# Induced-set attention and a SwiGLU block on one core: Newton roots, one set of PSUM banks, and a new instruction order

## The chip, the core and the metric

The kernel runs on one core of a Trainium2 chip. The core has a matmul engine (TensorE, PE in the profile, with its weight loads as PEld), a vector engine (VectorE, DVE), an activation engine (ScalarE, ACT), a general engine (GpSimd, POOL) and a sequencer that here only issues transfers (SyncE, SP). Each engine takes its own instructions strictly in the order in which the program gives them, and waits on semaphores for the others. The metric is the device time of one execution in microseconds; lower is better.

## The reference

There are four batches of 12416 rows of 128 numbers. Each goes through two attention steps with 32 learned rows, and the result, taken as 49664 rows, through a gated block of width 1536:

```python
def mab(q, kv):
    s = scale * (q @ kv.transpose(0, 2, 1))
    s = s - s.max(-1, keepdims=True)
    a = np.exp(s)
    a /= a.sum(-1, keepdims=True) + 1e-09
    return a @ kv
h = mab(I, x)                       # I: the 32 learned rows, for each batch
x = mab(x, h).reshape(B * S, D)     # 49664 x 128
rms = np.sqrt(np.mean(x * x, axis=-1, keepdims=True) + 1e-06)
xn = x / rms * rms_g
g = xn @ w_gate                     # 128 x 1536
silu = g * (1.0 / (1.0 + np.exp(-g)))
return silu * (xn @ w_val) @ w_out  # 1536 x 128
```

All inputs are random. The weights come as float64 and are rounded to fp32 on the chip.

## The kernel before

**Blocks.** Each batch is cut into seven sets of columns (five of 2048 rows, one of 1920, one of 256), and these into 25 units: twenty of 512 rows, four of 480, one of 256. Each unit goes through the 12 slices of 128 of the inner width. That is 25 x 12 = 300 blocks a batch and 1200 in all. One block is a gate matmul (`gate`, line 682), SiLU on ACT (`silu`, 692; for some blocks a tanh on ACT, 689, and a product on DVE, 702), a value matmul (`value`, 710), their product on DVE (`times_value`, 724) and the projection onto 128 outputs. Weights of gate and value are folded with the attention's 32 rows into stacks `sg` and `sv` (lines 485 and 504), so that the attention's output itself is never formed: the moving operand `a` is the normalised attention weight, split in a high and a low half.

**Three kinds of projection.** A block's letter in the string `sorts` chooses its kind:

- P, plain: the product goes to SBUF, and one full fp32 matmul with `wo` (line 781, `project_plain`; it appears as two matmul records) adds it to the unit's output sum in PSUM.
- S, split: the product u stays in its PSUM bank. ACT makes a rounded high part (`high`, 737), DVE the scaled rest (`low`, 743). Two fp32r matmuls put high and low parts in the bank of the upper sum (`project_two`, 769 and 770). POOL adds high and low parts in place (`add_in_place`, 789), and a third fp32r matmul (`project_third`, through 781) adds that to the output sum.
- D: like S, with the product in SBUF, the rest on POOL (`low_of_u`, 750) and a second ACT step (`high_down`, 756).

The first 26 blocks (`EARLY`) are plain whatever the string says. When a unit's matmuls are done, ACT takes the upper sum (`take_upper`, 822), DVE adds the output sum (`finish`, 834) and transposes it (842), and SP stores it in four transfers (855).

**Attention for the next batch** runs between the blocks of the present one: transposes of x (323), scores (340), maxima (352 to 362), exponentials on ACT (371, 473), sums (392), the 32 rows h, their products with the weights (485), second scores (340, 458), row maxima and their subtraction (462, 466; on POOL, or on DVE for the first set). For each set a chain called `seam` normalises: a transpose (540), a matmul with the rows' Gram matrix (544), a product (550), sums (554, 555), the root, its product with the weights (564, POOL), a transpose (568) and the two halves (574, 580). The root is one instruction on POOL:

```python
def root():
    rs = st["rs"] = numbers("rs")
    nc.gpsimd.tensor_tensor(out=rs, in0=st["ms"], in1=mhalf[rows, 0:n], op=ALU.pow)   # line 560
```

**Memory.** The eight PSUM banks are divided: five (`ps_gv`) for gates, values, products that stay in PSUM and all of the attention; two (`ps_acc`) for output sums; one (`ps_u`) for upper sums. Split factors have 19 places in SBUF, named by the string `holders`.

**Order.** It is written out. A first stage, the string `ORDER`, handles batch 0's attention and the rounding of the first third of the weights (lines 256 to 286). A second (`early`) ties the rest of the rounding, the stacks and the second scores to the first 26 blocks by block number. The remaining order is the string `program` of some 10,500 letters: g, s, v, m, p, h, l, n, e, q, d, r for the steps above, E, F, T, O for a unit's end, a for the transfers that gather `a`, and a dot for the next step of attention, whose number stands in `taken`. Where several blocks wait for the same step, the oldest is taken. Which bank a matmul gets stands in the string `banks`.

Of the kernel before, what the change touches and what calls it, by code (L numbers as in the profile page):

```python
# [23 lines left out]
def kernel(  # L24
# [10 lines left out]

# [47 lines left out]
    outp = pool("outp", 2)  # L117
    ps_gv = pool("ps_gv", 1, space=PSUM)
    ps_acc = pool("ps_acc", 2, space=PSUM)
    ps_u = pool("ps_u", 1, space=PSUM)  # L120
# [41 lines left out]
    mhalf = const.tile([P, 16], F32, name="mhalf")  # L162
# [24 lines left out]
    def warm(n):  # L187
        ps = ps_acc.tile([P, 512], F32, name="acc")
        for _ in range(n):
            nc.tensor.matmul(ps[:, 0:P], ident[:], ident[:], start=True, stop=True)  # L190

    warm(7)
    ps = ps_gv.tile([P, 512], F32, name="gv", tag="gv4")
# [25 lines left out]
    w0 = {}  # L219

    def rounding(i, c):
# [4 lines left out]
        def put():  # L226
            if i < 2:
                nc.sync.dma_start(out=w32[i][c][:], in_=st["dst"])
            if unread:
                fetch_raw(*unread.pop(0))  # L230
# [11 lines left out]
        def power():  # L242
            if i < 2:
                t = (xnp.tile([P, 512], F32, name=f"xn{2 * c - 1 + i}") if c else
                     silp.tile([P, 512], F32, name="silu") if i else halves.tile([P, 512], F32, name="lo"))
                w0[i, c] = t[:]
                dst = st["dst"] = w0[i, c]
            else:
                dst = st["dst"] = wo.rearrange("p j c -> p (j c)")[:, ts(c, 512)]
# [16 lines left out]
        def upper():  # L266
            if wide:
                f = st["f"] = outp.tile([P, 512], I32, name="o")
                nc.vector.tensor_scalar(out=f[:], in0=st["high"], scalar1=0xFFFFF, scalar2=None, op0=ALU.bitwise_and)
# [11 lines left out]
        def lower():  # L281
            if wide:
                e, f = st["e"], st["f"].bitcast(F32)
                nc.vector.scalar_tensor_tensor(out=f[:], in0=st["low"].bitcast(U32), scalar=2.0 ** -52, in1=f[:],
                                               op0=ALU.mult, op1=ALU.add)
                nc.gpsimd.tensor_tensor(out=st["dst"], in0=f[:], in1=e.bitcast(F32)[:], op=ALU.mult)  # L286
            put()
# [6 lines left out]
    NB, turn, turns, works, factors = 5, [0], [], [int(c) for c in "01201212"], []  # L294

    def bank():
# [5 lines left out]
        return ps_gv.tile([P, 512], F32, name="gv", tag=f"gv{n}")  # L302
# [5 lines left out]
    def attention(b, load_next):  # L308
# [41 lines left out]
        def max1():  # L350
            t = st["own"] = small.tile([P, R, NS], F32, name="owns")
            nc.vector.tensor_tensor(out=t[:], in0=st["gmx"][:].unsqueeze(1).to_broadcast((P, R, NS)),
# [88 lines left out]
        def square_h():  # L441
# [3 lines left out]
            stacks[b] = [stk.tile([P, F], F32R, name=n) for n in ("sg", "sv")]  # L445
# [18 lines left out]
        def sub_max(s):  # L464
            n, v, mx = per2[s], weights(b, s), st["mx2", s]
            (nc.gpsimd if s else nc.vector).tensor_tensor(
# [29 lines left out]
        def place(i, k):  # L496
            half = st["halves", i][k // 2]
            for c in range(NC):
                nc.sync.dma_start(out=stacks[b][i][ts(k, m), ts(c, 512)].bitcast(F32), in_=half[ts(c, m), :].bitcast(F32))

        def stack_of(i, c):
# [3 lines left out]
            nc.scalar.copy(out=stacks[b][i][:, ts(c, 512)], in_=ps[:])  # L505
# [22 lines left out]
    def seam(b, s):  # L528
# [29 lines left out]
        def root():  # L558
            rs = st["rs"] = numbers("rs")
            nc.gpsimd.tensor_tensor(out=rs, in0=st["ms"], in1=mhalf[rows, 0:n], op=ALU.pow)  # L560
# [21 lines left out]
        return [turn_a, square, times, scale, root, apply, turn_b, split, lower]  # L582

    def gather(b, u):
# [4 lines left out]
        a = moving[b, u] = (xnp.tile([P, 512], F32R, name="xn0") if (b, u) == (0, 2) else  # L589
# [4 lines left out]
    def split_wo(step):  # L594

        if not step:
            kws["first"] = xnp.tile([P, half + NK, C], F32R, name=f"xn{full - 1}")
            rings = [xnp.tile([P, RING * 512], F32R, name=f"xn{full - 4 + n}") for n in range(3)]
            kws["room"] = [ring[:, ts(n, 512)] for ring in rings for n in range(RING)][:3 * RING - 2]
            kws["wide"], kws["own"] = rings[2], {}  # L600

        def part(kind, g):
            n = kind * NK + g * half
            t = kws["first"][:, n:n + half, :] if n < half + NK else kws["more"][:, n - half - NK:n - NK, :]
            return t, t.bitcast(F32)

        def scaled(kind, g, mul, src=None):
            to, now = part(kind, g)
            nc.scalar.activation(to, now if src is None else src, AF.Copy, scale=mul)

        for g in range(2):
            one = wo[:, g * half:(g + 1) * half, :]
            at = step - g
            if at == 0:
                scaled(0, g, 1.0 - 2.0 ** -13, one)
            if at == 1:
                nc.gpsimd.tensor_tensor(out=part(1, g)[0], in0=one, in1=part(0, g)[1], op=ALU.subtract)
            if at == 3:
                scaled(1, g, 4096.0)
            if at == 4:  # L620
                nc.gpsimd.tensor_tensor(out=part(2, g)[0], in0=part(0, g)[1], in1=part(1, g)[1], op=ALU.subtract)
            if at == 6:
                scaled(0, g, -4096.0)

    def last_of(step):

        n = NJ - NK
        room = rings_last()
        one, (whi, wlo, ws) = wo[:, NK:NJ, :], (room[:, ts(kind, n), :] for kind in range(3))
# [11 lines left out]
    def rings_last():  # L641
        return kws["wide"][:, 2 * 512:4 * 512].rearrange("p (k c) -> p k c", c=C)

    def weight_of(kind, j):
        if j >= NK:
            return rings_last()[:, kind * (NJ - NK) + j - NK, :]
        n = kind * NK + j
        return kws["first"][:, n, :] if n < half + NK else kws["more"][:, n - half - NK, :]

    blocks, kinds = [], []  # L650
    at_unit = {}
    lists = {name: [] for name in "hlneqdDrRpx"}
# [3 lines left out]
    def unit_of(b, u):  # L656
        if (b, u) not in at_unit:
            s, q = units[u]
            at_unit[b, u] = {"T": per2[s] * m, "a": moving.pop((b, u)), "left": NJ, "q": 0, "acc": None,
                             "k": sum(kind != "P" for kind, one in zip(kinds, blocks) if one[:2] == (b, u)), "ups": None,  # L660
                             "o": None}
# [6 lines left out]
    def factor():  # L668
        return up.tile([P, 512], F32, name="u", tag=f"u{factors.pop(0)}")

    def room():
        n = factors.pop(0)
        if n < HELD and n not in kws["own"]:
            kws["own"][n] = up.tile([P, 512], F32R, name="u", tag=f"u{n}")[:]
        return kws["own"][n] if n < HELD else kws["room"][n - HELD]
# [20 lines left out]
    def gate_times():  # L696
        n = lists["x"].pop(0)
# [14 lines left out]
    def times_value():  # L712
# [5 lines left out]
        else:  # L718
            factor_of[n] = {"u": factor()[:, 0:T]}
# [7 lines left out]
    def high():  # L727
        n = lists["h"].pop(0)
# [11 lines left out]
    def low():  # L740
        n = lists["l"].pop(0)
# [5 lines left out]
    def low_of_u():  # L747
        n = lists["n"].pop(0)
# [4 lines left out]
    def high_down():  # L753
        n = lists["e"].pop(0)
# [4 lines left out]
    def project_two():  # L759
        n = min(lists["q"], key=lambda n: blocks[n][:2])  # L760
        lists["q"].remove(n)
# [3 lines left out]
        if one["ups"] is None:  # L765
            one["ups"] = ps_u.tile([P, 512], F32, name="u3")
        ups = one["ups"][:, 0:T]
        last = one["q"] == one["k"] - 1
        nc.tensor.matmul(ups, weight_of(0, j), halves_in_turn(t["hi"]), start=not one["q"], stop=False)  # L769
        nc.tensor.matmul(ups, weight_of(1, j), halves_in_turn(t["lo"]), start=False, stop=last)  # L770
        one["q"] += 1
        lists["D" if kinds[n].islower() else "d"].append(n)

    def project(n, lhsT, rhs, step2):
# [3 lines left out]
        if one["acc"] is None:  # L778
            one["acc"] = ps_acc.tile([P, 512], F32, name="acc")
        to = one["acc"][:, 0:T]  # L780
        nc.tensor.matmul(to.rearrange("p (n h) -> p h n", h=2) if step2 else to, lhsT, rhs, start=one["left"] == NJ,  # L781
                         stop=one["left"] == 1)
# [3 lines left out]
    def add_in_place():  # L786
        n = lists["d"].pop(0)
# [4 lines left out]
    def add_by_transfer():  # L792
        n = lists["D"].pop(0)
        t = factor_of[n]
        nc.gpsimd.dma_start(out=t["lo"].bitcast(F32), in_=t["hi"].bitcast(F32), accum_op=ALU.add)
        lists["R"].append(n)

    def project_third(name):
        n = lists[name].pop(0)
        project(n, weight_of(2, blocks[n][2]), halves_in_turn(factor_of[n]["lo"]), False)  # L800

    def project_plain():
        n = lists["p"].pop(0)
# [4 lines left out]
    flat = [(b, u) for b in range(B) for u in range(NU)]  # L808
# [5 lines left out]
    def take_upper():  # L814
        b, u = next_unit("E")
        one = unit_of(b, u)
        T = one["T"]
        assert one["q"] == one["k"]
        if not one["k"]:
            return  # L820
        o = one["o"] = outp.tile([P, 512], F32, name="o")
# [3 lines left out]
    def finish():  # L825
# [4 lines left out]
        if not one["k"]:  # L830
            one["o"] = outp.tile([P, 512], F32, name="o")
        whole = one["o"][:, 0:T].rearrange("p (q n) -> p q n", q=R)
        if one["k"]:
            nc.vector.tensor_tensor(out=whole, in0=in_order(one["acc"][:, 0:T]), in1=whole, op=ALU.add)
        else:
            nc.vector.tensor_copy(out=whole, in_=in_order(one["acc"][:, 0:T]))
# [30 lines left out]
    def parts(i, c, *engine):  # L867
        one = weight[i, c]
        one["power"]()
        one["power_number"](*engine)  # L870
        one["upper"]()
        one["upper_number"](*engine)

    def join(i, c):
        weight[i, c]["sign"]()
        weight[i, c]["lower"]()

# [3 lines left out]
        s1 t32 m1 t30 s2 a32 t33 t31 p00 P00 v30 u00 m2 own0 g00 Uv00 mB0 t40 l00 t42 nb0 a31 a33 t41 a40 v42 e0 t43  # L881
        s3 t51 a41 v43 s4 m3 e2 t52 t53 r0 t50 a51 m4 t60 own1 mB1 e1 a53 a50 a52 h0 r2 nb1 e3 p10 P10 r1 u10 U10 a60
        s5 h1 r3 m5 p20 e4 g10 s6 m6 h2 ls0 own2 mB2 u20 p11 nb2 ls1 r4 e5 least share r5 h3 h4 e6 ls2 shared fold h5
        r6 h6 l10 by0 by1 by2 P20 g20 u11 turn_h hT sc0z sc1z U20 l20 T0z rm0z sub0z ex0z T1z gram ta0z w7 sq0z rm1z
# [605 lines left out]
```

## Time and profile before

| | us |
|---|---|
| three runs | 1513.41, 1515.77, 1516.26 |
| their median | 1515.77 |
| the profiled execution: first to last instruction | 1513.0 |
| TensorE busy | 1496.2 |
| VectorE busy | 1454.9 |
| GpSimd busy | 1362.4 |
| ScalarE busy | 1268.6 |
| weight loads busy | 1090.8 |
| first gate matmul starts | 47.3 |

The granted clock of TensorE is 0.998 on the mean. The page gives no time of the profiled execution other than its span; the median is 2.8 us above it. A busy time is the time in which at least one instruction of the engine is open. Matmuls overlap in the records: each is shown with its time through the array, and the next starts before it ends. So a busy share of TensorE near 100% does not say at what rate it works; the distance from one start to the next does. In the groups of the profile, "out<-in" are the program's names of the tiles, then come partitions x elements and the count, busy time and mean length, and the engine's idle time before these instructions with what ended it. In the rows of windows each engine's busy time is followed by its number of instructions; behind the engines stand the granted clock, the share of the transfer engines, and GB/s.

### The profile page before, as it was taken

What the parts mean: (1) busy time and instruction counts of PE and PEld (TensorE: products, weight loads), DVE (VectorE), ACT (ScalarE), POOL (GpSimd) and SP (SyncE); (2) the same over time, 40 slices, a digit from 0 to 9 for tenths busy, and PEclk for the clock granted to TensorE, in tenths of its full rate; (3) what the DMA queues carried; (4) which work ended last, traced back from release to release, by engine and by line L of the source; (5) the groups of instructions that cost most, each with busy time, mean ns of one, the idle gap of its engine ahead of it and who ended that gap; (6) DMA issues with size and microseconds to landing.
All of it is one profiled execution on the core that took longest, in us unless ns stands there. A gap on an engine that the chain in (4) does not pass through costs nothing.

```text
span 1513.0 us, 25789 instructions
## 1 busy us (share of the span) xinstructions
PE 1496.2 (99%) x7138; PEld 1090.8 (72%) x7138; DVE 1454.9 (96%) x2570; ACT 1268.6 (84%) x2457; POOL 1362.4 (90%) x1114
## 2 busy tenths in 40 slices
PE   9999999999999999999999999999999999999998
PEld 6547667766777767766777777776678777777787
DVE  6989999999999999989999999999999999999997
ACT  5778888878889889887988888887888988888886
POOL 1369998998989998999999999898889999999998
PEclk9999999999999999999999999999999999999999
DMA  7386226444352323554444233633212121221222
GB/s 285 93 136 118 39 36 127 116 89 78 64 101 37 74 56 71 108 119 74 84 70 74 44 68 63 145 78 66 45 34 43 36 35 36 42 43 29 42 41 34
DMA packets 389327, 112.55 MB, mean 74 GB/s; under 512 B 365088, under 2 KB 369728, under 8 KB 386624
## 3 DMA queue, kind: packets, MB, share of 16 engines
q1 hardware_dynamic: 388592, 110.83, 36.8%
q8 instruction: 57, 0.93, 0.3%
q14 instruction: 86, 0.70, 0.2%
q10 hardware_dynamic: 592, 0.08, 0.0%
HBM read 53.95 MB, written 27.00 MB: 54 GB/s over the span
## 4 chain that ended last, share of the span: by engine, by line
PE 96%; DVE 2%; ACT 1%; issue 1%; POOL 0%; DMA 0%; SPq 0%; ACTq 0%; POOLq 0%
PE acc L781 32%; PE gv L682 17%; PE gv L710 17%; PE u L769 11%; PE u L770 11%; PE gv L340 3%; PE gv L544 1%; PE gv L392 1%; PE gv L907 1%; PE gv L485 0%; PE acc L190 0%; PE gv L504 0%; DVE u L724 0%; DMA out_dram<-o 0%; POOL xn L286 0%
## 5 line engine op out<-in xcount | busy, mean ns | idle before, releaser
L692 ACT ACTIVATE silu<-gv 128x512 f32<-128x512 f32 (+2 forms) x1173 | 664.1, 590 | 132.9 <-PE gv L682 120.8
L789 POOL TENSOR_TENSOR u<-xn,u 128x512 fp32r<-128x512 f32 (+2 forms) x399 | 495.6, 1258 | 24.3 <-PE u L770 22.8
L710 PE MATMUL gv<-a,sv 128*128 128x512 f32 (+2 forms) x1188 | 472.5, 398 | 2.2 <-ACT silu L692 2.1
L682 PE MATMUL gv<-a,sg 128*128 128x512 f32 (+2 forms) x1188 | 472.9, 399 | 0.1
L789 POOL TENSOR_TENSOR xn<-xn,xn 128x512 fp32r<-128x512 f32 (+2 forms) x340 | 424.9, 1262 | 29.2 <-PE u L770 21.0
L724 DVE TENSOR_TENSOR gv<-silu,gv 128x512 f32<-128x512 f32 (+2 forms) x653 | 424.3, 674 | 10.8 <-PE gv L710 8.1
L737 ACT ACTIVATE xn<-gv 128x512 fp32r<-128x512 f32 (+2 forms) x656 | 383.4, 593 | 45.1 <-DVE gv L724 35.0
L781 PE MATMUL acc<-u,wo 128*128 128x512 f32 (+2 forms) x768 | 376.5, 576 | 0.0
L724 DVE TENSOR_TENSOR u<-silu,gv 128x512 f32<-128x512 f32 (+2 forms) x520 | 336.5, 657 | 13.3 <-PE gv L710 5.5
L769 PE MATMUL u<-xn,xn 128*128 128x512 f32 (+2 forms) x778 | 294.3, 379 | 0.0
L682 PEld LDWEIGHTS gv<-a,sg 128*128 128x128 f32 x1188 | 224.6, 189 | 90.2 <-issue 18.1
L710 PEld LDWEIGHTS gv<-a,sv 128*128 128x128 f32 x1188 | 224.4, 189 | 84.1 <-issue 18.9
L743 DVE SCALAR_TENSOR_TENSOR xn<-xn,gv 128x512 fp32r<-128x512 f32 (+2 forms) x333 | 218.7, 663 | 2.9 <-ACT xn L737 2.3
L743 DVE SCALAR_TENSOR_TENSOR u<-xn,gv 128x512 fp32r<-128x512 f32 (+2 forms) x323 | 211.9, 663 | 3.1 <-ACT xn L737 2.0
L781 PEld LDWEIGHTS acc<-u,wo 128*128 128x128 f32 x768 | 143.8, 190 | 28.5 <-issue 12.0
L769 PEld LDWEIGHTS u<-xn,xn 128*128 128x128 f32 x778 | 147.2, 189 | 20.1 <-issue 2.7
L781 PE MATMUL acc<-xn,more 128*128 128x512 f32 (+2 forms) x347 | 160.3, 464 | 0.0
L781 PE MATMUL acc<-u,more 128*128 128x512 f32 (+2 forms) x328 | 154.6, 475 | 0.0
L750 POOL TENSOR_TENSOR xn<-u,xn 128x512 fp32r<-128x512 f32 (+2 forms) x80 | 101.3, 1268 | 6.5 <-ACT xn L734 4.7
L734 ACT ACTIVATE xn<-u 128x512 fp32r<-128x512 f32 (+2 forms) x156 | 97.9, 628 | 9.4 <-DVE u L724 5.8
L756 ACT ACTIVATE xn<-xn 128x512 fp32r<-128x512 f32 (+2 forms) x156 | 97.9, 628 | 5.6 <-POOL u L750 3.5
L789 POOL TENSOR_TENSOR xn<-xn 128x512 fp32r<-128x512 f32 (+2 forms) x73 | 92.0, 1262 | 9.6 <-PE u L770 9.1
(213 smaller groups left out, 1840.3 us busy)
## 6 DMA issues: line engine op xcount, KB each, us to landing
out_dram<-o SPq DMA_DIRECT2D x320, 64.0 KB, 2.0
xT<-in_x_dram SPq DMA_DIRECT2D x60, 256.0 KB, 4.7
xn<-in_x_dram SPq DMA_DIRECT2D x60, 256.0 KB, 5.0
a<-hi SPq DMA_DIRECT2D x156, 64.0 KB, 2.0
a<-lo SPq DMA_DIRECT2D x156, 64.0 KB, 2.0
xn<-in_x_dram SPq DMA_DIRECT2D x5, 1024.0 KB, 9.4
xn<-w SPq DMA_DIRECT2D x18, 256.0 KB, 3.8
out_dram<-o SPq DMA_DIRECT2D x64, 60.0 KB, 2.0
```

What stands on the lines that cost most here:

```text
L682: nc.tensor.matmul(g[:, 0:T], stacks[b][0][:, ts(j, P)], halves_in_turn(one["a"][:, 0:T]), start=True, stop=True)
L692: nc.scalar.activation(sl[:, 0:T], gates.pop(n)[:, 0:T], AF.Silu)
L710: nc.tensor.matmul(v[:, 0:T], stacks[b][1][:, ts(j, P)], halves_in_turn(one["a"][:, 0:T]), start=True, stop=True)
L724: nc.vector.tensor_tensor(out=to, in0=sl[:, 0:T], in1=v[:, 0:T], op=ALU.mult)
L734: nc.scalar.activation(hi, t["u"], AF.Copy, scale=1.0 - 2.0 ** -13)
L737: nc.scalar.activation(hi, t["u"], AF.Copy, scale=-(1.0 - 2.0 ** -13) * 2.0 ** -12)
L743: nc.vector.scalar_tensor_tensor(out=t["lo"], in0=t["hi"].bitcast(F32), scalar=4096.0, in1=t["u"], op0=ALU.mult, op1=ALU.add)
L750: nc.gpsimd.tensor_tensor(out=t["lo"], in0=t["u"], in1=t["hi"].bitcast(F32), op=ALU.subtract)
L769: nc.tensor.matmul(ups, weight_of(0, j), halves_in_turn(t["hi"]), start=not one["q"], stop=False)
L770: nc.tensor.matmul(ups, weight_of(1, j), halves_in_turn(t["lo"]), start=False, stop=last)
L781: nc.tensor.matmul(to.rearrange("p (n h) -> p h n", h=2) if step2 else to, lhsT, rhs, start=one["left"] == NJ, stop=one["left"] == 1)
L789: nc.gpsimd.tensor_tensor(out=t["lo"], in0=t["hi"].bitcast(F32), in1=t["lo"].bitcast(F32), op=ALU.add)
```

## The change

1. **Roots.** In `seam` the power on POOL gives way to a first guess (ACT, on the bits of the number) and three Newton steps, each with two instructions on ACT and two on POOL. They work on at most 16 numbers in each partition. Batch 0's first set keeps the power.
2. **Banks.** One pool of eight banks serves gates, values, attention, output sums and upper sums. The string `banks` names one of eight for each use, sums included.
3. **Factors.** Places of factors in SBUF are called by their name in `holders` for all three kinds of block; the weights of the third projection are split in five groups (4, 4, 1, 1 and 2 slices) in place of three, each with its own place in the list.
4. **The list.** Weight rounding, from the second third on, stands as steps of its own in the list, with `lower` parted into `lower`, `join` (POOL) and `put` (the store); so do stacks and second scores. `EARLY` and the function `early` are gone: all 1200 blocks take their kind from `sorts`.
5. **Choice.** A string `picks` tells, at each step, which of the waiting blocks is taken; before, it was the oldest.
6. **Engines.** `max1` goes from DVE to POOL, and so does `sub_max` of a batch's first set.
7. **The order** is a new string of 11,331 letters. Kinds: P 384 before and 324 after, S 657 and 685, D 159 and 191. Tanh blocks: 27 and 7. ACT's table loads: 16 and 18. Transfers issued on SP: 1081 in both.

The core of the diff:

```diff
-    ps_gv = pool("ps_gv", 1, space=PSUM)
-    ps_acc = pool("ps_acc", 2, space=PSUM)
-    ps_u = pool("ps_u", 1, space=PSUM)
+    psum = pool("psum", 1, space=PSUM)
...
-    mhalf = const.tile([P, 16], F32, name="mhalf")
+    mhalf = small.tile([P, 16], F32, name="rt", bufs=1)
...
                 nc.vector.scalar_tensor_tensor(out=f[:], in0=st["low"].bitcast(U32), scalar=2.0 ** -52, in1=f[:],
                                                op0=ALU.mult, op1=ALU.add)
+
+        def join():
+            if wide:
+                e, f = st["e"], st["f"].bitcast(F32)
                 nc.gpsimd.tensor_tensor(out=st["dst"], in0=f[:], in1=e.bitcast(F32)[:], op=ALU.mult)
-            put()
...
-        return ps_gv.tile([P, 512], F32, name="gv", tag=f"gv{n}")
+        return psum.tile([P, 512], F32, name="gv", tag=f"b{n}")
...
         def max1():
             t = st["own"] = small.tile([P, R, NS], F32, name="owns")
-            nc.vector.tensor_tensor(out=t[:], in0=st["gmx"][:].unsqueeze(1).to_broadcast((P, R, NS)),
+            nc.gpsimd.tensor_tensor(out=t[:], in0=st["gmx"][:].unsqueeze(1).to_broadcast((P, R, NS)),
...
-            (nc.gpsimd if s else nc.vector).tensor_tensor(
+            nc.gpsimd.tensor_tensor(
                 out=v, in0=v, in1=mx.unsqueeze(2).to_broadcast((mx.shape[0], n, m)), op=ALU.subtract)
...
-        def root():
+        def seed():
             rs = st["rs"] = numbers("rs")
-            nc.gpsimd.tensor_tensor(out=rs, in0=st["ms"], in1=mhalf[rows, 0:n], op=ALU.pow)
+            nc.scalar.activation(rs.bitcast(I32), st["ms"].bitcast(I32), AF.Copy, bias=float(0x5F3759DF), scale=-0.5)
+
+        def newton(step):
+            def square_root():
+                t = st["t"] = small.tile([P, 16], F32, name="rt", bufs=1)[rows, 0:n]
+                nc.scalar.activation(t, st["rs"], AF.Square)
+            def times_mean():
+                nc.gpsimd.tensor_tensor(out=st["t"], in0=st["t"], in1=st["ms"], op=ALU.mult)
+            def from_three():
+                nc.scalar.activation(st["t"], st["t"], AF.Copy, bias=1.5, scale=-0.5)
+            def next_root():
+                nc.gpsimd.tensor_tensor(out=st["rs"], in0=st["rs"], in1=st["t"], op=ALU.mult)
...
-        return [turn_a, square, times, scale, root, apply, turn_b, split, lower]
+        return [turn_a, square, times, scale, seed, *newton(0), *newton(1), *newton(2), apply, turn_b, split, lower]
...
     def low():
-        n = lists["l"].pop(0)
+        n = lists["l"].pop(choices.pop(0))
...
         if one["ups"] is None:
-            one["ups"] = ps_u.tile([P, 512], F32, name="u3")
+            one["ups"] = bank()
...
         if one["acc"] is None:
-            one["acc"] = ps_acc.tile([P, 512], F32, name="acc")
+            one["acc"] = bank()
```

Left out of it are the strings, the list entries of `later` that name the new steps, the function `early` and unused parts that went with it.

## The prediction

> **What bounds the kernel now.** I read the engines' totals first, then the windows, then the waits, and last the instructions in order of time. In the fence below stand two rows of the profile's page: busy time by engine, and the chain that ended last.
>
> ```profile
> PE 1496.2 (99%) x7138; PEld 1090.8 (72%) x7138; DVE 1454.9 (96%) x2570; ACT 1268.6 (84%) x2457; POOL 1362.4 (90%) x1114
> ...
> PE 96%; DVE 2%; ACT 1%; issue 1%; POOL 0%; DMA 0%; SPq 0%; ACTq 0%; POOLq 0%
> ```
>
> The chain is TensorE's almost throughout, but DVE is at 96% beside it, so neither can be relieved alone. The windows say where each is full. I cut the span where TensorE starts its 0th, 50th, 100th ... gate matmul (line 682), so that a window is 50 of the 1200 blocks:
>
> ```profile
> 47.30:122.50 75.20, 70.43 (x255) 40.08 (x256) 67.90 (x112) 53.73 (x97) 42.83 (x36) 0.98 0.67 121
> ...
> 432.90:489.50 56.60, 56.59 (x252) 42.37 (x250) 56.32 (x99) 49.07 (x96) 52.25 (x45) 1.00 0.35 60
> ...
> 617.80:686.70 68.90, 68.90 (x355) 48.23 (x354) 62.52 (x104) 56.96 (x113) 66.57 (x53) 1.00 0.48 103
> ...
> 1221.90:1278.40 56.50, 56.50 (x235) 43.48 (x235) 55.91 (x95) 50.39 (x96) 55.97 (x45) 1.00 0.22 41
> ```
>
> After the bounds and the length come PE, PEld, DVE, ACT and POOL. In the second row PE and DVE are full; in the third PE and POOL; in the last, of the fourth batch, all three at 99%. The first loses time on every engine. The clock column is 1.00, so the clock plays no part. Next, the costs of one instruction, from the timeline (start, length), and from the groups by shape (count, busy us, mean ns, idle before):
>
> ```profile
> 608.60 1.02 PE L781 MATMUL acc<-u,wo 128*128 128x512 f32 x2
> 609.21 0.62 PE L682 MATMUL gv<-a,sg 128*128 128x512 f32 x1
> 609.67 0.38 PE L710 MATMUL gv<-a,sv 128*128 128x512 f32 x1
> 609.88 0.38 PE L769 MATMUL u<-xn,xn 128*128 128x512 f32 x1
> ...
> 1003.23 1.31 POOL L750 TENSOR_TENSOR xn<-u,xn 128x512 fp32r<-128x512 f32 x1
> 1004.47 1.31 POOL L789 TENSOR_TENSOR xn<-xn,xn 128x512 fp32r<-128x512 f32 x1
> ```
>
> ```profile
> L560 POOL TENSOR_TENSOR rs<-ms,mhalf 128x16 f32<-128x16 f32 x19 | 55.4, 2918 | 5.0 <-DVE ms L555 4.9
> L452 ACT ACTIVATE gram<-gv 32x32 f32<-32x32 f32 x16 | 3.0, 185 | 1.0 <-PE gv L447 0.9
> L184 POOL CAST u<-ident 128x32 fp32r<-128x32 f32 x4 | 0.7, 209 | 0.1
> ```
>
> Starts count, not lengths, since neighbours overlap. A reduced-precision (fp32r) matmul of 512 columns takes 609.88 - 609.67 = 0.216 us. From the plain fp32 product at 608.60 to the value at 609.67 are 1.07 us, less 0.216 for the gate between: a plain product costs 0.86 us, a split one, of three fp32r matmuls, 0.65. POOL starts 512-wide operations 1.24 us apart; pairs in the timeline give DVE 0.60 (two in 1.27 us, one 0.67 long) and ACT 0.48 to 0.52 (two in 1.10, one 0.60). Summing every instruction of the list at such spacings gives PE 1447 us, DVE 1434, POOL 1361, ACT 1165. So TensorE's 99% hides about 66 us in which it worked slower than it can.
>
> **The change, part by part.** Counts come from comparing the two instruction lists.
>
> *Plain into split.* Plain blocks fall from 384 to 324, split ones rise from 816 to 876 (kind S 657 to 685, kind D 159 to 191). By width the 60 are 46 of 512 columns, -6 of 480, 20 of 256. TensorE saves 0.21 us for 512, about 0.20 for 480 and 0.10 for 256: 9.7 - 1.2 + 2.1 = 10.6 us, all on the path while TensorE binds.
>
> *What that loads elsewhere.* POOL's fp32r operations rise by 78 of 512 (1.24 us), 23 of 256 (0.69), and fall by 5 of 480 (1.17): 96.7 + 15.9 - 5.9 = +107. ACT gets 80 x 0.50 + 23 x 0.30 - 5 x 0.5 = +44. DVE gets 28 subtractions, line 743 (18 x 0.60 - 7 x 0.57 + 17 x 0.34 = +12.6), and loses 20 gate products of line 702 as tanh blocks go from 27 to 7 (20 x 0.60 = -12).
>
> *Roots.* 27 powers, line 560, leave POOL: 55.4 + 11.0 + 6.5 = -73 us by their rows (128x16, 128x15, 32x8). In come 27 seeds and 162 steps on ACT and 162 products on POOL, at most 16 elements wide, which the trace of before does not have. On ACT the nearest row is L452 at 0.185: 189 x 0.19 = +36 us; the other end, L737's spacing of 0.48, would make 91. ACT has about 350 us to spare by spacing, and both ends fit into it. On POOL the nearest is the 128x32 cast, 0.209 long and 0.15 apart: 162 x 0.15 = +24 us. The lower end is the 128x16 memset (0.111): +18; the upper the 32x8 power (1.637): 265, unlikely, since the power computes per element and a product does not; twice the cast, 0.3, would be +49. I take 24.
> [...]
>
> *Moves.* The maxima's product (L352, 2.8 us) and three subtractions (L466, 2.1) go from DVE to POOL (about 4); the output weights are split in five groups instead of three (-6 on POOL, none on the path); two table loads more (1.28 each) lie in ACT's room. Loads and stores keep their number (1081 issues on SP's queue); those of the next batch's x move with the order, and out_dram's 2 us landings have two buffers as before. Sums: PE -10.6, DVE -2 (-4 by row lengths), ACT +84, POOL 107 - 73 + 24 + 4 - 6 = +58 with the rest of the moves.
>
> *Banks.* Before, five PSUM banks serve gates, values and attention, two the output sums, one the upper halves. Now all eight serve all. Its price is below nothing or nil: POOL waits 54 us in total for line 770 in the rows below, and the 24 us that blocks 50 to 899 lose are in stages in which attention takes banks.
>
> ```profile
> ACT silu L692 <- PE gv L682: 120.8, 217, 3.0
> ...
> POOL xn L789 <- PE u L770: 30.1, 33, 3.2
> POOL u L789 <- PE u L770: 23.9, 22, 3.3
> ```
>
> *Weight rounding and the first blocks.* The first 26 blocks were plain by decree, with rounding tied to block numbers; now the order decides. Nothing is added.
>
> **The sum.** By spacings, window for window, I took the most loaded engine of each 50 blocks.
> Blocks 50 to 1149 before: PE 1296, DVE 1288, POOL 1259, sum of the window maxima 1304, time 1331. After: PE 1285, DVE 1280, POOL 1302, sum of maxima 1305. So what TensorE is spared POOL takes up, and the floor stays. What can change is the loss above it. Blocks 900 to 1149 (no attention for a next batch) lose 2.2 us on 284.7, 0.8%; blocks 50 to 899 lose 24.8 on 1019.7, 2.4%. I take 1.7% there, between the two, because of the three more banks and the free choice among waiting blocks, and since POOL's work can wait longer than TensorE's.
> First gate at 47.3, as before (that order is nearly unchanged). Blocks 0 to 49: 75.2 us now against 63.5 of PE load; after, DVE has most with 67; 69 taken. Blocks 50 to 899: 1020.3 x 1.017 = 1037.6. Blocks 900 to 1149: 284.3 x 1.008 = 286.6. The end: 59.1 + 0.5. Together 1500.1 against 1513.0. The median of the runs, 1515.8, lies 2.8 above the profiled span, so 1502.9; I say 1503.
>
> **The rivals.**
> *GpSimd becomes the bound and stalls (slower).* After block 50 POOL has 1358 us of work in what were 1390 us; 32 us of new idleness, 1.3 us for each of the 25 roots there, eat all room. A Newton chain crosses between ACT and POOL twelve times, POOL works in order, and behind a waiting product stand the adds that TensorE's third matmul needs. One POOL wait is 0.9 us (30.1/33). If two of a root's six products wait, that is 25 x 1.8 = 45 us: with POOL's 1358, the 117 before block 50, 5 at the end and the 2.8 makes 1528. Against it: in the new list other POOL work stands between most steps. It decides from 1.3 us a root.
> *No gain: DVE holds it.* DVE is full in most windows and loses only 2 us. Same losses and same first blocks: 47.3 + 75.2 + 1020.3 x 1.024 + 286.6 + 59.6 + 2.8 = 1516. [...]
> *More gain.* All of blocks 50 to 899 at 0.8%: 1494. Also the way it goes if eight banks do nothing, but the first blocks run at their load: 1510, inside the forecast's spread.
>
> **How the numbers follow.** Forecast (gain of 5 to 20 us) 0.50; more 0.11; no gain 0.16; GpSimd 0.23. A measurement can tell 0.2%, 3 us, from no change. Faster takes the first two and the edge of the third: 0.62; same 0.14; slower 0.24. The range goes from the larger gain, 1490, to near GpSimd's case, 1525: less than 2 in 10 is outside.
>
> **What would show it.** Right: PE's busy time some 10 us lower, POOL at 1415 to 1435 and 94% or more of the span, gate 50 at 114 to 118 us, small products on POOL at 0.15 to 0.25 us, DVE's idle time less in the windows of 65 us and more. Wrong: POOL waiting for ACT in the Newton lines by more than 30 us (GpSimd's case); DVE at 99% with gate 50 still at 122 (no gain); or small products at 0.5 us and more, 57 us on POOL.

## The result and the profile after

The changed kernel takes 1521.73 us (median of five runs, 1520.86 to 1524.80); the kernel before, on the same chip, 1515.77 (1513.41 to 1517.65). The ratio is 1.0051, its 95% interval 1.0036 to 1.0066: slower by 0.5%, where 1503 and a gain had been forecast. The profiled execution lasts 1518.8 us against 1513.0.

First the engines and the chain in the page of the changed kernel:

```profile
PE 1492.1 (98%) x7198; PEld 1107.9 (73%) x7198; DVE 1454.5 (96%) x2572; ACT 1327.1 (87%) x2748; POOL 1426.9 (94%) x1351
...
PE 92%; SPq 3%; DVE 2%; ACT 1%; DMA 1%; issue 1%; POOL 0%; DVEq 0%; ACTq 0%; POOLq 0%
```

POOL is where the sum had it (1415 to 1435, 94%). But SPq, the queue in which SP issues transfers, stands in the chain with 3%, where it had 0%; TensorE's share fell from 96% to 92%. The windows at the same gates as before:

```profile
46.70:125.50 78.80, 71.82 (x264) 40.67 (x264) 70.31 (x119) 64.70 (x126) 56.41 (x56) 0.96 0.78 115
434.60:490.10 55.50, 55.50 (x241) 41.17 (x241) 55.06 (x97) 50.73 (x107) 54.83 (x55) 1.00 0.53 91
616.60:679.00 62.40, 62.40 (x379) 49.25 (x378) 60.49 (x104) 55.48 (x115) 61.61 (x56) 1.00 0.54 115
1225.70:1282.40 56.70, 56.70 (x239) 43.85 (x237) 56.59 (x96) 50.84 (x104) 56.20 (x51) 1.00 0.18 33
```

The third window, 68.9 us before, now takes 62.4, and DVE's idle time in it fell from 6.4 to 1.9 us. A single window also changes because attention work moved into others; blocks 300 to 549 together fell from 316.0 us to 309.2, so this stretch is better filled. The first window is the one that got worse, 78.8 us against 75.2, and its clock column is 0.96. The waits tell of what (us in total, times, longest):

```profile
ACT silu L665 <- PE gv L655: 73.4, 157, 6.0
...
POOL u L761 <- PE gv L742: 10.4, 11, 5.1
...
POOL xn L761 <- PE gv L742: 8.9, 15, 1.9
...
ACT o L785 <- DMA out_dram<-o: 7.3, 2, 6.4
...
DVE xT L300 <- DMA xT<-in_x_dram: 5.6, 2, 4.0
```

POOL's waits for TensorE's split products fell from 54 us to 19.3, ACT's for gates from 120.8 to 73.4. New are waits for transfers, few and long: ACT for a store (6.4 us), DVE for a load (4.0). The next fence follows the longer one through the timeline, SP's own rows first (start, length, and how many issues in a row), then the rows of 117 to 121 us with what ended the idle time before each:

```profile
96.71 17.82 SPq L110 DMA_DIRECT2D xT<-in_x_dram  x12
114.64 3.56 SPq L813 DMA_DIRECT2D out_dram<-o  x4
...
117.37 0.71 DVE L300 STREAM_TRANSPOSE xT<-xT 128x512 f32<-128x512 f32 x1 [4.04 <-DMA xT<-in_x_dram]
...
120.14 0.60 ACT L785 ACTIVATE o<-gv 128x512 f32<-128x512 f32 x1 [6.37 <-DMA out_dram<-o]
...
120.79 0.79 PE L683 MATMUL gv<-a,sv 128*128 128x512 f32 x1 [4.29 <-ACT o L785]
```

SP's rows stand in the order of the list. Twelve loads of the next batch's x take 17.8 us to issue, 1.5 us each. Behind them stands the first unit's store: its first issue starts at 114.64, 0.1 us after the last load's has ended. There are two output buffers, used in turn, so the upper sum of the third unit on ACT (L785) needs the buffer of that store: ACT waits 6.4 us, and TensorE for ACT 4.3. The same happens at 787 us with the gathers of `a`: SP is busy without a pause from 763 to 791 us, and TensorE's next unit waits for the last transfer:

```profile
777.03 5.55 SPq L99 DMA_DIRECT2D xn<-in_x_dram  x4
782.63 2.03 SPq L479 DMA_DIRECT2D sg<-wlo  x3
784.71 0.59 SPq L110 DMA_DIRECT2D xT<-in_x_dram  x1
785.58 3.85 SPq L593 DMA_DIRECT2D a<-hi  x1
789.53 0.54 SPq L593 DMA_DIRECT2D a<-lo  x1
...
792.67 0.55 PE L655 MATMUL gv<-a,sg 128*128 128x256 f32 x1 [5.55 <-DMA a<-lo]
```

Each of these two idle stretches has a second price. A window at the end of each shows the granted clock at 0.50, and the clock's own record has it there for 6.83 us from 119.16 and from 791.58, up to 3.4 us lost each time:

```profile
119.20:125.80 6.60, 4.23 (x9) 3.12 (x10) 5.16 (x9) 5.57 (x11) 2.09 (x2) 0.50 0.71 166
126.00:136.00 10.00, 10.00 (x44) 7.73 (x43) 9.30 (x17) 9.06 (x18) 9.00 (x8) 1.00 0.30 55
791.70:798.30 6.60, 5.63 (x15) 4.36 (x16) 2.54 (x5) 2.58 (x6) 2.00 (x2) 0.50 0.76 119
```

Summed over the trace, from one matmul's start to the next and less their usual spacing, gaps above 0.7 us behind the first gate come to 18.2 us after and 7.9 before; the halved clock, leaving out the last microseconds of the run, costs 6.8 after and 1.7 before. Together that is about 25 against 10, and part of it lies where the other engines use the pause.

One theory from this: the change gained about what was predicted, and the order of SP's queue took it back (queue theory). Its rival: TensorE, DVE and POOL are all at 94 to 98%, what one is spared another takes, and the transfers would be late for any reason (coupling theory).

### The profile page after: what moved, and what is told of

It is laid out like the page before. It is cut to its first block, busy times and chain, and to the rows that moved or that the text cites. A ratio compares the mean times of both kernels' runs of the same rounds, so it can differ in the third digit from the quotient of the medians.

```text
span 1518.8 us, 26130 instructions
## 1 busy us (share of the span) xinstructions
PE 1492.1 (98%) x7198; PEld 1107.9 (73%) x7198; DVE 1454.5 (96%) x2572; ACT 1327.1 (87%) x2748; POOL 1426.9 (94%) x1351
## 4 chain that ended last, share of the span: by engine, by line
PE 92%; SPq 3%; DVE 2%; ACT 1%; DMA 1%; issue 1%; POOL 0%; DVEq 0%; ACTq 0%; POOLq 0%
PE gv L753 28%; PE gv L655 17%; PE gv L683 16%; PE gv L741 12%; PE gv L742 12%; PE gv L317 3%; SPq L110 2%; PE gv L526 1%; PE gv L369 1%; PE gv L854 1%; DMA a<-lo 1%; SPq L593 0%; DMA xT<-in_x_dram 0%; ACT silu L665 0%; PE gv L153 0%
## 5 line engine op out<-in xcount | busy, mean ns | idle before, releaser
L665 ACT ACTIVATE silu<-gv 128x512 f32<-128x512 f32 (+2 forms) x1193 | 686.4, 590 | 105.8 <-PE gv L655 73.4
L761 POOL TENSOR_TENSOR u<-xn,u 128x512 fp32r<-128x512 f32 (+2 forms) x327 | 401.6, 1239 | 10.9 <-PE gv L742 10.1
L761 POOL TENSOR_TENSOR xn<-xn,xn 128x512 fp32r<-128x512 f32 (+2 forms) x309 | 384.9, 1255 | 4.8 <-PE gv L742 4.1
L753 PE MATMUL gv<-u,wo 128*128 128x512 f32 (+1 forms) x648 | 326.0, 587 | 0.2
L716 DVE SCALAR_TENSOR_TENSOR u<-xn,gv 128x512 fp32r<-128x512 f32 (+2 forms) x268 | 172.9, 650 | 2.1 <-ACT xn L710 0.9
L761 POOL TENSOR_TENSOR xn<-xn 128x512 fp32r<-128x512 f32 (+2 forms) x131 | 164.9, 1262 | 5.7 <-PE gv L742 4.8
L741 PE MATMUL gv<-xn,xn 128*128 128x512 f32 (+2 forms) x400 | 153.8, 385 | 0.0
L761 POOL TENSOR_TENSOR u<-u 128x512 fp32r<-128x512 f32 (+2 forms) x109 | 137.2, 1262 | 1.1 <-PE gv L655 0.7
L753 PEld LDWEIGHTS gv<-u,wo 128*128 128x128 f32 x648 | 120.4, 190 | 23.8 <-issue 7.9
L741 PE MATMUL gv<-xn,more 128*128 128x512 f32 (+2 forms) x344 | 136.0, 395 | 0.0
L753 PE MATMUL gv<-u,xn 128*128 128x512 f32 (+2 forms) x253 | 97.5, 395 | 0.1
```

Of the source, the lines that this page charges most:

```text
L665: nc.scalar.activation(sl[:, 0:T], gates.pop(n)[:, 0:T], AF.Silu)
L716: nc.vector.scalar_tensor_tensor(out=t["lo"], in0=t["hi"].bitcast(F32), scalar=4096.0, in1=t["u"], op0=ALU.mult, op1=ALU.add)
L741: nc.tensor.matmul(to, weight_of(0, j), halves_in_turn(t["hi"]), start=not one["q"], stop=False)
L761: nc.gpsimd.tensor_tensor(out=t["lo"], in0=t["hi"].bitcast(F32), in1=t["lo"].bitcast(F32), op=ALU.add)
```

## The experiments

All times are medians of at least four runs; ratios are to the kernel before on the same chip, where its own median was between 1513.6 and 1515.8 us. So a difference between two rows in us is good to some 2 us.

| kernel | us | ratio | 95% interval |
|---|---|---|---|
| changed kernel | 1521.73 | 1.0051 | 1.0036 to 1.0066 |
| 1 all loads spread | 1504.14 | 0.9934 | 0.9922 to 0.9947 |
| 2 first batch's loads only | 1515.67 | 1.0013 | 1.0004 to 1.0022 |
| 3 later batches' loads only | 1511.05 | 0.9982 | 0.9973 to 0.9992 |
| 4 power back | 1566.05 | 1.0349 | 1.0333 to 1.0364 |
| 5 changed kernel, loads in long rows | 1505.28 | 0.9937 | 0.9925 to 0.9950 |
| 6 as 1, Newton in one step | 1595.18 | 1.0542 | 1.0520 to 1.0563 |
| 7 kernel before with Newton in one step | 1601.74 | 1.0581 | 1.0566 to 1.0597 |
| 8 as 1, seed only | 1503.61 | 0.9928 | 0.9914 to 0.9941 |
| 9 as 1, fewer matmuls | 1497.13 | 0.9887 | 0.9873 to 0.9900 |
| 10 as 1, fewer transposes | 1501.67 | 0.9918 | 0.9905 to 0.9932 |
| 11 as 1, all three relieved | 1491.27 | 0.9848 | 0.9835 to 0.9862 |
| 12 kernel before, loads in long rows | 1510.67 | 0.9978 | 0.9969 to 0.9987 |

### 1 to 3: the same work, with the loads elsewhere in the list

Only letters of `program` and numbers of `taken` move: the 28 loads `xT` of each batch's x, two row loads of batch 3 (`xn`, four transfers each) and seven transposes of x on VectorE. The numbers below are the count of gates issued when each of the 28 loads is (batch 2 is alike):

```diff
 batch 1
- 6 7 8 9 9 10 27 29 30 31 32 32 32 33 33 35 36 37 38 40 40 42 43 44 44 47 50 67
+ 6 9 12 15 18 20 23 25 27 30 33 36 46 49 52 55 58 61 64 67 70 74 78 82 85 88 91 95
 batch 3
- 523 524 525 525 526 530 531 543 544 546 547 549 550 557 558 559 567 574 577 577 583 585 590 604 626 629 647 675
+ 523 528 531 539 540 543 547 554 558 559 565 569 572 575 583 587 587 594 597 601 603 607 615 615 623 626 627 631
```

> The changed kernel with nothing but transfers (and seven transposes of x that read them) moved in the list: the 28 loads of batch 1's x, which stand in gates 27 to 50, are placed one by one over gates 6 to 95; those of batches 2 and 3 at least four blocks apart and each behind a store or gather. Every arithmetic instruction stays. Queue theory (SP's queue delays the gathers and stores, TensorE idles, and its clock is halved for some us afterwards): the idle times above 0.7 us after the first gate sum to 18 us and two halvings cost 3.4 each; most of that goes, 15 to 22 us, so 1500 to 1507 us, below the kernel before (1515.8). Coupling theory (PE, DVE and POOL are each at 94 to 98%, and what one is spared another takes): moving transfers changes nothing, 1519 to 1525.

> Of the former edit only the part for batch 1's loads (in the first 95 blocks). Queue theory: the idle times at 67.7, 115.9 and 120.8 us (1.9 + 4.5 + 1.4) and one halving of the clock (3.4) go: 8 to 11 us less than the changed kernel, 1511 to 1514, with gate 50 at 114 to 118 us. Coupling theory: within 3 us of 1521.7, gate 50 still at 122 or later.

> Of the first edit only the part for the loads of batches 2 and 3. Queue theory: the idle times at 407.5, 786.8, 796.9 and 1011.1 us (2.7 + 5.7 + 0.8 + 1.3) and one halving (3.4) go: 9 to 13 us less than the changed kernel, 1509 to 1513; together with the part for the first batch it adds up to the first edit's gain. Coupling theory: within 3 us of 1521.7.

Measured: 17.6 us less than the changed kernel with all loads spread, 6.1 with the first batch's, 10.7 with the others'. The two parts add up to 16.8. All three follow the queue theory; the second falls short of its 8 to 11. In the page of kernel 1 the instructions are the same in number as in the changed kernel, and in its first window, in the second fence, the clock is whole. Over its whole trace, TensorE's gaps above 0.7 us come to about 3 us in place of 18, and the clock is not halved before the last microseconds:

```profile
PE 1487.4 (99%) x7198; PEld 1103.1 (73%) x7198; DVE 1453.0 (97%) x2572; ACT 1327.5 (88%) x2748; POOL 1425.6 (95%) x1351
```

```profile
46.70:116.60 69.90, 69.27 (x263) 39.49 (x262) 67.82 (x115) 63.73 (x124) 55.66 (x55) 1.00 0.50 89
```

In kernel 2 gate 50 comes at 117.2 us instead of 125.5, 8.3 earlier as expected, but gate 300 only 2.8 earlier. At 402 us an idle gap of 3.3 us stands that had been 2.7, and a halving of the clock for 3.4 us follows it, which the changed kernel does not show there. The rest may be that DVE and POOL use a pause to get ahead; that is not shown.

### 5 and 12: the list untouched, the loads in longer runs

```diff
-        nc.sync.dma_start(out=xT[b, s][ts(k, m), :].rearrange("p (w c) -> p w c", c=m),
-                          in_=xrows[ds(b * N + start[s], P * per[s]), ts(k, m)].rearrange("(i w) c -> i w c", i=m))
+        nc.sync.dma_start(out=xT[b, s][ts(k, m), :],
+                          in_=xrows[ds(b * N + start[s] + k * m * per[s], m * per[s]), :].rearrange("(i w) c -> i (w c)", i=m))
```

> The changed kernel with its list untouched, but each load of x for batches 1 to 3 reads the same 256 KB as runs of 8 KB instead of runs of 128 bytes (so the numbers arrive in another order, and the output is that of permuted inputs). If it is the number of short packets that fills the queue and holds up what stands behind the clumped loads: the issue of a clumped load falls from 2.0 us to 0.7 or less, the idle times of 4.5 us at 116 and 5.7 us at 787 shrink below 2 us, no halving of the clock, and 1503 to 1510 us with not one instruction moved. If it is the place in the list alone (so many issues ahead, whatever they carry): issue lengths stay, and the time stays within 3 us of 1521.7. Coupling theory: 1521.7 too.

> The kernel before with its list untouched and, as in the earlier experiment on the changed kernel (1505.3 us), each load of x for batches 1 to 3 reading its bytes in runs of 8 KB instead of 128 bytes (other order of the numbers, so the output is that of permuted inputs). It asks what the rest of the change is worth once the transfers are out of the way in both. The kernel before has the same twelve loads in a row ahead of a store (86 to 104.5 us), TensorE idles of 1.8, 2.4, 1.0 and 1.3 us near its loads and one halving of the clock of 3.4 us (1.7 lost). If the change without the queue is worth the predicted 12.7: no gain here, 1513 to 1516. If the kernel before pays for its clump as well: 3 to 8 us less, 1507 to 1512, and the change is then worth 2 to 7.

Measured: 1505.3 for the changed kernel and 1510.7 for the kernel before. SP's rows around the first clump, in kernel 5 (changed list), in the kernel before, and in kernel 12 (list before):

```profile
91.71 8.01 SPq L110 DMA_DIRECT2D xT<-in_x_dram  x12
105.91 2.66 SPq L813 DMA_DIRECT2D out_dram<-o  x4
```

```profile
86.02 18.50 SPq L147 DMA_DIRECT2D xT<-in_x_dram  x12
104.62 3.63 SPq L855 DMA_DIRECT2D out_dram<-o  x4
```

```profile
80.13 9.72 SPq L147 DMA_DIRECT2D xT<-in_x_dram  x12
100.43 2.66 SPq L855 DMA_DIRECT2D out_dram<-o  x4
```

Twelve issues in the same place and with the same bytes take 8.0 us instead of 17.8, and the store behind them no longer waits. So it is not the number of issues ahead but what they carry: a load of 256 KB in runs of 128 bytes (2048 of them) is issued in 0.6 us when none of its kind is just ahead of it (1.3 and 1.5 in two places of the changed kernel), and mostly in 1.1 to 2.3 when others are (2.7 at most). Two details of the expectation for kernel 5 missed: at 775 us a gap of 2.6 us stays (5.7 in the changed kernel), and one halving of 3.4 us follows it. By the profile SP waits there, before it issues the gathers, for the row loads `xn` ahead of them (3.7 us in all); this edit leaves those loads as they are.

The second fence was there to be read before the prediction: the kernel before pays for a clump too, by 2.9 us (just under the 3 to 8 of that theory). TensorE's gap behind it is 2.4 us there, against 4.7 in the changed kernel, and nothing like the 5.7 us at 787 follows. With these transfers out of the way in both, the rest of the change is worth 1510.7 - 1505.3 = 5.4 us (6.2 by the two ratios), and the queue costs the changed kernel 1521.7 - 1505.3 = 16.4.

### 4, 6 and 7: what the roots cost

The power at the seed's place (4, the first two lines), and the whole chain at the seed's place (6, the last three lines; the twelve later places are left empty). Kernel 7 has the same chain in the kernel before, in place of the power:

```diff
-            nc.scalar.activation(rs.bitcast(I32), st["ms"].bitcast(I32), AF.Copy, bias=float(0x5F3759DF), scale=-0.5)
+            nc.gpsimd.tensor_tensor(out=rs, in0=st["ms"], in1=mhalf[rows, 0:n], op=ALU.pow)
...
+            for k in range(3):
+                for one in newton(k):
+                    one()
```

> The changed kernel with the power on POOL back in place of the Newton steps: 27 powers (2.0 to 2.9 us, 73 us in all) stand where the seeds stand; the 162 products on POOL (29 us at their spacing of 0.18) and 189 steps on ACT are gone; the rest of the list is as it is. POOL's work rises by some 44 us to 1470. Queue theory: POOL still has room in parts of the span, but not in the windows in which it is full, so 5 to 40 us slower than the changed kernel, most likely 20. Theory that the roots' many small steps are what cost the gain (crossings between ACT and POOL): 10 us or more faster than the changed kernel.

> The kernel with all loads spread (1504.1 us), with a root's seed and its twelve Newton instructions issued one behind the other at the place of the seed, instead of a step at a time between other work. It prices the rival of the prediction in which GpSimd waits for ScalarE. That rival's 0.9 us for each of the six crossings to POOL: some 5 us for each of 25 roots, of which POOL's fullness passes on most, 60 to 130 us more. If a crossing costs only the two instructions' own lengths (about 0.2 us each, 13 in a chain: POOL stands for 2 us a root): 10 to 50 us more, taken 30.

> The kernel before with the 27 powers of the seams as a seed and twelve Newton instructions at the same place in its list, one behind the other; nothing else of the change. POOL loses 73 us and gets 29 and its waits for ScalarE. If TensorE's and VectorE's load bounds the kernel before, and POOL only in some windows: within 6 us of the kernel before, so that the roots alone give nothing and only pay with the extra split blocks. If POOL bounded it: 5 to 25 us less. If the crossings cost 0.9 us: POOL stands for 5 us a root in place of 2.9, 10 to 40 us more.

Measured: the power costs 44.3 us, above the 5 to 40 expected; POOL's busy time rises by 41.5 (to 1468.4). The chain in one step costs 91.0 us in the list of kernel 1, which lies in the range of the 0.9 us crossings, and 87.2 in the list before, over any of the ranges. The groups of kernel 6 tell how the chain runs; the last column is the engine's idle time before these instructions:

```profile
L556 POOL TENSOR_TENSOR rt<-rt,ms 128x16 f32<-128x16 f32 (+2 forms) x81 | 17.6, 218 | 24.1 <-ACT rt L553 21.7 <-DVE u L703 1.9 <-DVE gv L703 0.3
...
L562 POOL TENSOR_TENSOR rs<-rs,rt 128x16 f32<-128x16 f32 (+2 forms) x81 | 17.6, 217 | 26.3 <-ACT rt L559 25.9 <-DVE gv L703 0.3
...
L553 ACT ACTIVATE rt<-rs 128x16 f32<-128x16 f32 (+2 forms) x81 | 17.4, 215 | 18.5 <-POOL rs L562 17.6
L559 ACT ACTIVATE rt<-rt 128x16 f32<-128x16 f32 (+2 forms) x81 | 17.4, 214 | 31.1 <-POOL rt L556 31.1
```

A chain takes 3.6 us from seed to last product (median of 27), and for that time both POOL and ACT do nothing else: POOL waits 50.4 us in total, 1.9 a root, ACT 49.6. The crossings themselves are 0.3 to 0.4 us each (25.9 us in 80 waits, 31.1 in 81), not 0.9.

That 27 x 3.6 = 96 us lies near the 91 is in part chance, for TensorE pays in two ways. Against kernel 1 its gaps above 0.7 us grow from 3 to 71 us, by 2.5 us a root. And many of them are followed by a halved clock: 15 times for 3.4 us in this trace, not once in kernel 1's before the last microseconds, which is up to 26 us. The granted clock says the same: 0.982 to 0.989 in the five runs of kernel 6 against 0.999 and 1.000. Kernel 7 has 12 such halvings, and kernel 4 has seven where the changed kernel has two. In the changed kernel the same products stand between other work and hardly wait:

```profile
L556 POOL TENSOR_TENSOR rs<-rs,rt 128x16 f32<-128x16 f32 x57 | 12.9, 227 | 0.9 <-ACT rt L553 0.7
L550 POOL TENSOR_TENSOR rt<-rt,ms 128x16 f32<-128x16 f32 x57 | 12.9, 226 | 0.9 <-ACT rt L547 0.8
```

So the roots gain by being parted, not by being Newton's: in these two lists, neither of which was made for it, the same instructions in one piece are worse than the power.

### 8 to 11: what binds once the queue is out of the way

```diff
 8: -        return [turn_a, square, times, scale, seed, *newton(0), *newton(1), *newton(2), apply, turn_b, split, lower]
 8: +        return [turn_a, square, times, scale, seed, *[nothing] * 12, apply, turn_b, split, lower]
 9: +        if last or n % 6:
 9:              nc.tensor.matmul(to, weight_of(1, j), halves_in_turn(t["lo"]), start=False, stop=last)
10: +        if leaving["T"] % 2:
10:              nc.vector.transpose(out=o[:, 0:T], in_=o[:, 0:T])
```

> The kernel with all loads spread (1504.1 us), without the twelve Newton steps of each root: the seed alone stands for the root, so the result is rougher, and POOL has 29 us less, ACT some 35. If POOL is the bound in the windows of batches 1 to 3 (it was the most loaded by spacings in those): 10 to 25 us less. If TensorE and VectorE hold it: within 3 us of 1504.

> The kernel with all loads spread (1504.1 us), in which every sixth block, where it is split, leaves out the matmul of its low part (the result is rougher): some 140 matmuls of 0.216 us, about 29 us off TensorE and nothing off any other engine. Together with the next two it asks which engine the kernel ends on, now that the queue is out of the way. TensorE as the bound, as the prediction had it: 15 to 29 us less. Coupling (the most loaded engine changes from window to window, and DVE or POOL is within 1 to 2% of TensorE in each): 0 to 6 us less.

> The kernel with all loads spread, without the transpose of the output in every second unit (those outputs are stored untransposed): about 48 instructions of 0.6 to 0.7 us, some 30 us off DVE and nothing off any other. DVE as the bound: 15 to 30 us less. Coupling, or TensorE as the bound: 0 to 6 us less.

> Both former edits and no Newton steps after the seeds: some 29 us off TensorE, 30 off DVE, 29 off POOL. Coupling: the three together give what none gives alone, 15 to 27 us less than 1504.1. If one engine were the bound, its own run would show as much as this one.

Against kernel 1: POOL relieved by 26.5 us of busy time gives 0.5 us, which is no measurable difference, DVE by 50 transposes (23.7 us of busy time) gives 2.5, TensorE by 135 matmuls (29 us at their spacing) gives 7.0, and the three together 12.9. For POOL and DVE that is the coupling theory's picture. TensorE's 7.0 lies between the two theories, over 0 to 6 and under 15 to 29. The three together fell short of 15 to 27 and give little more than the 10.0 of the three single runs, so coupling alone does not explain it: some 16 us of the relief found no way to the end. What holds it was not found: the written order, which was made for the full work and which each engine keeps, is the candidate, but no run took it away.

Kernels 4 and 8 stand side by side: 26.5 us off POOL give nothing, 41.5 more cost 44.3. In kernel 4 TensorE's third matmuls wait for POOL's adds, which they do neither in the changed kernel nor in kernel 1:

```profile
PE gv L752 <- POOL u L760: 11.5, 12, 2.5
PE gv L752 <- POOL xn L760: 5.5, 6, 1.9
```

So the reading is that slivers of 0.2 us hold up nothing, while 2.9 us in one piece hold up the adds for TensorE.

## Why the prediction was wrong, and where it was right

By stages, in profiled executions (us):

| | before | forecast | after | 1 spread | 5 long rows | 12 before, long rows |
|---|---|---|---|---|---|---|
| to the first gate | 47.3 | 47.3 | 46.7 | 46.7 | 46.6 | 46.9 |
| blocks 0 to 49 | 75.2 | 69 | 78.8 | 69.9 | 69.6 | 71.1 |
| blocks 50 to 899 | 1044.5 | 1037.6 | 1044.5 | 1037.1 | 1038.0 | 1044.8 |
| blocks 900 to 1149 | 286.9 | 286.6 | 287.4 | 287.6 | 287.6 | 287.0 |
| the end | 59.1 | 59.6 | 61.4 | 61.1 | 61.8 | 59.2 |
| span | 1513.0 | 1500.1 | 1518.8 | 1502.4 | 1503.6 | 1509.0 |

**The step that failed** is the sentence in "Moves": "Loads and stores keep their number (1081 issues on SP's queue); those of the next batch's x move with the order, and out_dram's 2 us landings have two buffers as before". The number was right, and so were the landings (2.1 us at the median), but the wait to be issued was not counted: the sum put the queue at nothing. A store and a gather wait behind what stands ahead of them in SP's queue, and the new list puts 20 of batch 1's 28 loads into gates 27 to 47, and loads of batch 3 ahead of the gathers at 787 us. That cost 16.4 us (kernel 5 against the changed kernel), more than the 12.7 forecast as the gain. No rival had it either; a wait for a transfer that takes the place of the one removed was nowhere priced. That the measured 1521.7 still lies in the stated range, 1490 to 1525, is luck: its upper end was set by a stall of GpSimd that did not happen.

**Two readings of the trace before** were off. "The clock column is 1.00, so the clock plays no part": its first row has 0.98. That is a halving for 3.4 us, behind a gap of 2.4 us at 109 us, just after the clump of loads; it was the sign of the cost that the change made larger. And the 66 us in which TensorE "worked slower than it can" are the span less the load: 17 of them are idle (1513.0 - 1496.2), and 49 stand in the busy time.

**Blocks 0 to 49.** "69 taken", from DVE's load of 67, was right as a load: 69.9 and 69.6 without the queue's stalls. What the trace of before lost there (75.2 against 63.5 of load) was in good part the same queue: with long rows it is 71.1. Of the 6 us counted as the change's, 1.5 are its own.

**Blocks 50 to 899.** Forecast 1037.6, a loss of 1.7% above the floor instead of 2.4%; 1037.1 and 1038.0 without the queue's stalls, which ate the 7 us in the changed kernel. The better filling stands: with long rows and the list before (12) the stage keeps its 1044.8. The floor does not stand as it was summed. It had POOL as the most loaded engine (1302 us in blocks 50 to 1149 against TensorE's 1285), yet kernel 8 takes 26.5 us off POOL and the stage stays at 1037.0, while kernel 9's matmuls bring it to 1031.9. So the closeness of the number is in part luck. Which of banks, free choice and order brings the filling was not parted; POOL's fewer waits for TensorE (54 to 19 us) fit all three.

**The end** was taken at +0.5 and is +2.0 to +2.7 in all three kernels with the new list. Behind gate 1150 every engine has more left to do there: TensorE is busy for 56.2 us after and 54.0 before, VectorE for 53.3 and 50.9, GpSimd for 55.3 and 52.9. So part of it is work that stood ahead of that gate before.

**The instructions' prices** held in the main. POOL's small products: 0.15 us taken, and without them (8) POOL's busy time is 26.5 us lower, 0.16 for each of 162. POOL's total: +58 forecast, 1426.9 - 1362.4 = +64.5; ACT's: +84 forecast, 1327.1 - 1268.6 = +58.5. TensorE's busy time fell by 4.1 us, and by 8.8 in kernel 1, for the 10 expected. ACT's steps were taken at 0.19; leaving 162 out takes 15.1 us from its busy time, 0.09 each. Their lengths, 214 and 215 ns in kernel 6, lie above the 185 of L452, from which the 0.19 was taken; as a price even that is too high, since neighbours overlap. The reason given for not pricing a product like a power, that "a product does not" compute per element, was wrong, though 24 us was near: POOL's products cost 1.24 us at 512 elements and 0.69 at 256, some 2 ns an element, the power 2.9 us at 16 and 1.6 at 8, some 160.

**The rivals.** GpSimd's stall did not happen: POOL waits for ACT in the Newton lines by about 2 us, not over 30. Its condition was well put (the steps must stand between other work) and its waiting of 1.8 us a root is what kernel 6 shows (1.9); its price, 45 us, was half of the 91. It counted POOL's waits alone; the 91 also hold ACT's standing still and up to 26 us of halved clock, and how these add up was not parted. "DVE holds it" came nearest in time, by another mechanism; gate 50 "still at 122" (it was 125.5) came from the queue, and kernel 10 gives DVE alone 2.5 us. That what TensorE is spared lies "all on the path" holds for about a quarter (7.0 of 29, kernel 9).

Kernel 1 is the version that beats both: 1504.14 us, 0.66% under the kernel before (0.53 to 0.78%).

## What to carry to other kernels

Count a moved transfer like any other moved instruction: list what the issuing queue holds ahead of each store and gather, with the issue times from the trace, before and after. Look for a clump of transfers in short runs with something urgent behind it: spreading it, or lengthening its runs, here gave 16 to 18 us, three times what the rest of the change is worth (5.4). Look for halved clock as well: behind 32 of 50 gaps of 2 to 3 us on TensorE it cost up to 1.7 us more. And put other work between the steps of a chain that crosses two engines: in one piece it held ACT and POOL for its full 3.6 us (kernel 6), and parted, in the changed kernel, 57 of its products waited 0.9 us in all.

## What the runs showed of the hardware

The issue of a 256 KB load in runs of 128 bytes took mostly 0.6 us with none of its kind just ahead of it (1.3 and 1.5 in two places) and up to 2.7 behind others, so the length of an issue row is not only the cost of issuing.

TensorE's clock fell to half after short idle gaps, but not after every one. Gaps are taken from one matmul's start to the next, less the usual spacing, behind the first gate, in all fourteen traces. A halved clock began within 4 us of the end of 32 of the 50 gaps of 2.0 to 3.0 us, of five of the seven of 3.1 to 3.8, and of all four of 4.7 to 6.0. Of the 19 of 1.5 to 2.0 us it followed two, one alone (1.8 us, kernel 6) and one close behind another gap; of the 31 of 1.0 to 1.5, none. In the kernel before it began 0.2 us behind the gap of 2.4, in the changed kernel 1.6 and 1.1 us ahead of the end of those of 4.7 and 5.7. Before the last microseconds of a run it lasted 3.4 us each time, and 6.8 behind the four longest and behind that pair. Why one of two gaps of like length is followed by it and the other not, no run here shows.
